# Banded attention and a gated MLP on one core: first weight loads on ScalarE's queue, one DMA queue in the plan, later second products, other buffer counts

## The chip, the cores and the metric

The kernel runs on one core of a Trainium2 chip. The metric is the time on the device in microseconds (us); one number is the median of several executions. The engines are TensorE (PE; its weight loads are listed apart as PEld), VectorE (DVE), ScalarE (ACT), GpSimd (POOL) and SyncE (SP), which here mostly issues DMAs.

## What is computed

Four batches, eight heads, 768 positions, head size 64. Each position attends to the first 4 positions (sinks) and to the last 128 positions. The result, as a matrix x of 3072 x 512, goes through an MLP of width 2048 with the Mish function between its two products.

```python
scores = scale * np.matmul(q, k.transpose(0, 1, 3, 2))
keep = is_sink | in_window
scores = np.where(keep, scores, -1e9)
a = softmax(scores); attn = np.matmul(a, v)
x = attn.transpose(0, 2, 1, 3).reshape(B * S, H * D)
h = x @ w_in                      # 3072x512 @ 512x2048
g = h * np.tanh(softplus(h))
out = g @ w_out                   # 3072x2048 @ 2048x512
```

The weights come as 64-bit numbers. The kernel turns them into float32 on the chip, from the two halves of each number, and splits each into a high and a low part.

## The kernel before

The 3072 rows are worked in 12 chunks of 256 rows. The first chunk of each batch (no rows ahead of it) comes first: these are chunks 0 to 3 in the order of work. A chunk has four pairs of heads (`pair`): products of q and k (line L387 for the first chunk of a batch, L390 for others, tiles `att`), mask and maximum on DVE (L398), exponential on ACT (L401), normalisation (L405 to L412), transposes on PE (L422), and the product with v (L440, L444).

The MLP of a chunk has eight steps (`step`), each for two of the 16 blocks of 128 hidden units. A step does its first products into the tile `hp` (L488; in "wide" steps L484 and L485, with high and low parts of x side by side, followed on DVE by a sum, L494), then a chain that alternates between ACT and DVE: exponential into the tile `u` (L497), minimum (L498), square (L499), logarithm (L500), exponential (L501), product into `n` (L502), high part `gh` (L252) and low part `gl` (L263 or L265). Then come twelve second products into two accumulators `acc` (L518). At a chunk's end the accumulators are copied out into tiles that also carry the tag `u` (L252, L254 or L537) and stored to `y` (L541). Chunks 0 to 2 go through their steps interleaved, in groups of two steps, since the weights become ready only little by little; chunks 3 to 10 run one after the other with wide steps; chunk 11 is again not wide.

Each block of weights is a DMA of 512 KB into one of three buffers `raw`, then seven or eight instructions on ACT, DVE and POOL: L288 or L289, L291, L292, L294, L296, the sum L299 or L300, the high part L252, the low part L263 or L265. After the weights, the same buffers carry pieces of k.

The order on every engine is set ahead of time by `Plan.solve`: a list scheduler with a duration for every task, a rank (`prio`), and a count of buffers by tag (`TAGS`). A task is put on the engine on which it can start first, lower rank first among equals. The engines then run exactly in this order. `emit` also puts matmuls on a zero tile (L613) into places where the plan leaves PE idle. In the plan a load takes 460 ns on SP and then 2000 ns plus 2.9 ns for each KB, whatever else is on its way. Loads that `body` issues ahead of the plan (tags in `EARLY`, lines L815 to L820) count as landed at a fixed time.

## Time and profile before

| | |
|---|---|
| median of 3 runs | 740.74 us (739.2 to 741.14) |
| the profiled execution's own time | 741.95 us |
| its span, first to last instruction | 740.2 us |
| PE busy | 723.7 us (98% of the span) |
| weight loads on PE | 609.2 us (82%) |
| DVE busy | 551.5 us (75%) |
| ACT busy | 579.5 us (78%) |
| POOL busy | 129.0 us (17%) |
| mean granted TensorE clock | 0.994 |

Busy time is the time in which an engine had an instruction under way, as a share of the span. PE's share includes the matmuls on the zero tile. What lies around the span in the execution's own time is 1.75 us.

### The profile page before, as it was taken

What the parts mean: (1) busy time and instruction counts of PE and PEld (TensorE: products, weight loads), DVE (VectorE), ACT (ScalarE), POOL (GpSimd) and SP (SyncE); (2) the same over time, 40 slices, a digit from 0 to 9 for tenths busy, and PEclk for the clock granted to TensorE, in tenths of its full rate; (3) what the DMA queues carried; (4) which work ended last, traced back from release to release, by engine and by line L of the source; (5) the groups of instructions that cost most, each with busy time, mean ns of one, the idle gap of its engine ahead of it and who ended that gap; (6) DMA issues with size and microseconds to landing.
All of it is one profiled execution on the core that took longest, in us unless ns stands there. A gap on an engine that the chain in (4) does not pass through costs nothing.

```text
span 740.2 us, 12968 instructions
## 1 busy us (share of the span) xinstructions
PE 723.7 (98%) x4466; PEld 609.2 (82%) x4466; DVE 551.5 (75%) x1415; ACT 579.5 (78%) x1293; POOL 129.0 (17%) x108
## 2 busy tenths in 40 slices
PE   7999999999999999999999999999999999999996
PEld 5578788898888888887888888888888888888995
DVE  5999989997677877668877768777777777764332
ACT  5999889778888778887778878787878778875753
POOL 1232122202042112321031130111111311100000
PEclk9999999999999999999999999999999999999999
DMA  6555334323353232223224224223313311100000
GB/s 185 172 176 154 109 120 137 121 105 88 88 149 88 73 96 89 73 75 93 75 57 127 75 57 126 58 62 109 88 44 91 97 45 34 48 18 1 31 1 33
DMA packets 48988, 64.12 MB, mean 87 GB/s; under 512 B 4880, under 2 KB 41744, under 8 KB 48912
## 3 DMA queue, kind: packets, MB, share of 16 engines
q1 hardware_dynamic: 48912, 63.20, 29.4%
q8 instruction: 37, 0.61, 0.4%
q14 instruction: 39, 0.32, 0.1%
HBM read 56.89 MB, written 6.29 MB: 85 GB/s over the span
## 4 chain that ended last, share of the span: by engine, by line
PE 72%; ACT 13%; DVE 10%; DMA 2%; issue 2%; SPq 0%; DVEq 0%; ACTq 0%
PE acc L518 29%; PE hp L484 12%; PE hp L488 9%; PE hp L485 6%; PE att L440 4%; PE att L390 4%; PE att L422 3%; ACT p L401 3%; PE att L444 2%; DVE n L494 2%; PE att L488 2%; ACT u L499 1%; ACT u L500 1%; ACT u L497 1%; ACT w L252 1%
## 5 line engine op out<-in xcount | busy, mean ns | idle before, releaser
L518 PE MATMUL acc<-w,gh 128*128 128x512 f32 x768 | 198.3, 396 | 1.5 <-ACT gh L252 1.1
L484 PE MATMUL hp<-w,w 128*128 128x512 f32 x512 | 191.9, 409 | 0.0
L518 PEld LDWEIGHTS acc<-w,gh 128*128 128x128 f32 x768 | 137.1, 189 | 30.6 <-ACT gh L252 4.4
L485 PE MATMUL hp<-w,w 128*128 128x256 f32 x512 | 143.1, 280 | 0.0
L484 PEld LDWEIGHTS hp<-w,w 128*128 128x128 f32 x512 | 96.3, 188 | 17.5 <-issue 0.2
L518 PE MATMUL acc<-w,gl 128*128 128x512 f32 x384 | 107.6, 395 | 0.0
L401 ACT ACTIVATE p<-p,nm 128x288 f32<-128x288 f32 (+1 forms) x192 | 95.6, 501 | 6.6 <-DVE nm L398 6.5
L494 DVE TENSOR_REDUCE n<-hp 128x256 f32<-128x512 f32 x128 | 87.6, 685 | 15.1 <-PE hp L485 14.6
L485 PEld LDWEIGHTS hp<-w,w 128*128 128x128 f32 x512 | 96.8, 189 | 0.6
L499 ACT ACTIVATE u<-u,bias 128x512 f32<-128x512 f32 x96 | 69.4, 724 | 34.4 <-DVE u L498 34.3
L398 DVE CUSTOM_DVE_ANT_0 p<-att,m 128x288 f32<-128x288 f32 (+2 forms) x192 | 75.2, 419 | 26.5 <-PE att L390 19.9
L488 PE MATMUL hp<-w,w 128*128 128x256 f32 x672 | 91.7, 288 | 1.9 <-DVE n L502 1.8
L488 PEld LDWEIGHTS hp<-w,w 128*128 128x128 f32 x672 | 86.0, 193 | 6.0 <-DVE n L502 2.4
L263 POOL TENSOR_TENSOR w<-raw,w 64x448 fp32r<-64x448 f32 x35 | 41.8, 1200 | 260.5 <-ACT w L252 115.5
L497 ACT ACTIVATE u<-n 128x512 f32<-128x512 f32 x64 | 40.4, 632 | 54.1 <-DVE n L494 54.0
L518 PEld LDWEIGHTS acc<-w,gl 128*128 128x128 f32 x384 | 70.9, 188 | 14.3
L498 DVE TENSOR_SCALAR u<-u 128x512 f32<-128x512 f32 x96 | 42.8, 446 | 47.2 <-ACT u L497 46.8
L252 ACT ACTIVATE gh<-n 128x512 fp32r<-128x512 f32 x94 | 58.8, 625 | 17.4 <-DVE n L502 16.8
L500 ACT ACTIVATE u<-u,bias 128x512 f32<-128x512 f32 x96 | 68.9, 719 | 1.8
L502 DVE SCALAR_TENSOR_TENSOR n<-u,n 128x512 f32<-128x512 f32 x64 | 44.5, 695 | 34.0 <-ACT u L501 33.8
L265 DVE TENSOR_TENSOR gl<-n,gh 128x512 fp32r<-128x512 f32 x75 | 53.3, 711 | 18.2 <-PE acc L518 12.9
L501 ACT ACTIVATE u<-u 128x512 f32<-128x512 f32 x96 | 60.2, 628 | 2.0
(86 smaller groups left out, 1076.1 us busy)
## 6 DMA issues: line engine op xcount, KB each, us to landing
raw<-k_p SPq DMA_DIRECT2D x64, 224.0 KB, 3.5
raw<-w_in SPq DMA_DIRECT2D x16, 512.0 KB, 3.6
raw<-w_out SPq DMA_DIRECT2D x16, 512.0 KB, 4.2
w<-q_p SPq DMA_DIRECT2D x64, 128.0 KB, 3.2
y<-u SPq DMA_DIRECT2D x24, 256.0 KB, 2.1
vt<-v_b SPq DMA_DIRECT2D x32, 192.0 KB, 2.5
vsr<-v_s SPq DMA_DIRECT2D x32, 128.0 KB, 2.3
ks<-k_p SPq DMA_DIRECT2D x16, 144.0 KB, 2.9
```

The source lines that it names most:

```text
L252: ways[ACT] = act_t(n, psum), lambda: nc.scalar.activation(dst(), src(), AF.Copy, scale=scale or 1.0)
L265: way = dve_t(n), lambda: nc.vector.tensor_tensor(dst(), a(), b(), ALU.subtract)
L398: a = add(r + .03 + .01 * e, {DVE: (dve_t(n) + 8, lambda st=st, pv=pv, nm=nm, e=e, mask=mask, n=n: nc.vector.tensor_tensor_reduce(out=pv() ...
L401: a = add(r + .05 + .01 * e, {ACT: (act_t(n, ptr=2), lambda pv=pv, nm=nm, sm=sm, e=e: nc.scalar.activation(pv(), pv(), AF.Exp, bias=nm.t[: ...
L484: yield nc.tensor.matmul(hp.t, wih[f].t[:, fs], xt, start=kt == 0, stop=False)
L485: yield nc.tensor.matmul(hp.t[:, 0, :], wil[f].t[:, fs], xt[:, 0, :], start=False, stop=kt == KT - 1)
L488: yield nc.tensor.matmul(hp.t[:, y, :], w_.t[:, fs], xt[:, z, :], start=kt == 0 and n_ == 0, stop=kt == KT - 1 and n_ == 2)
L494: hs.append(add(r + .3 + .1 * y, {DVE: (dve_t(2 * T), lambda y=y, hp=hp: nc.vector.tensor_reduce(m.t[:, y, :], hp.t.rearrange("p z t -> p ...
L499: a = add(r + .52, {ACT: (act_t(N, ptr=1), lambda: nc.scalar.activation(u.t, u.t, AF.Square, bias=self.one))}, [a], [u])
L500: a = add(r + .53, {ACT: (act_t(N, ptr=1), lambda: nc.scalar.activation(u.t, u.t, AF.Ln, bias=self.half, scale=0.5))}, [a], [u])
L501: a = add(r + .54, {ACT: (act_t(N), lambda: nc.scalar.activation(u.t, u.t, AF.Exp, scale=-1.0))}, [a], [u])
L518: yield nc.tensor.matmul(acc[t].t, g_.t[:, y, ts_], w_.t, start=new and n_ == 0, stop=done)
```

## The change

There are four parts. (1) The first three loads of weights are issued by ACT, ahead of its table load, and no longer by SP behind the loads of k, q and v. (2) The plan keeps one line of loads: each load starts 1500 ns after its issue or when the one before it is through, takes 4.5 ns for each KB, and is usable 300 ns later; the preloaded weights count as landed at 2400, 4800 and 7200 ns instead of 3000, 6000 and 9000. (3) The second products of wide steps get a rank that is 0.2 later. (4) `ks` and `qh` (k and q of the chunks at the start of a batch) have three buffers instead of two, and the third pair's loads are issued ahead of the plan; `u` has two buffers instead of three. What is computed is the same.

```diff
--- before.py
+++ after.py
@@ -51,7 +51,8 @@
 WARM, SPARE, ROOM = 14, 250, 4
 ZERO = 224
 SPL = 1.5
-EARLY = {"ks": ([P, 2 * PITCH], F32, 0), "qh": ([P, T], F32, 0), "vt": ([P, 2, 3, D], F32, 0), "raw": ([P, 512, 2], I32, 3000)}
+LINE0, LINE, SLOW = 3000, 4.5, .2
+EARLY = {"ks": ([P, 2 * PITCH], F32, 0), "qh": ([P, T], F32, 0), "vt": ([P, 2, 3, D], F32, 0), "raw": ([P, 512, 2], I32, 2400)}
 SH, QUICK = 1.0, 2
 
 
@@ -93,13 +94,13 @@
 
 
 class Task:
-    __slots__ = ("prio", "ways", "deps", "bufs", "new", "ready", "left", "start", "end", "eng", "outs", "room")
+    __slots__ = ("prio", "ways", "deps", "bufs", "new", "ready", "left", "start", "end", "eng", "outs", "room", "size")
 
     def __init__(self, prio, ways, deps, bufs, new):
         self.prio, self.ways, self.deps, self.bufs, self.new = prio, ways, deps, bufs, new
         self.ready, self.left, self.outs = dict.fromkeys(ways, 0.0), 0, []
         self.start = self.end = self.eng = None
-        self.room = 0.0
+        self.room, self.size = 0.0, 0
 
 
 class Plan:
@@ -137,7 +138,7 @@
             for d in t.deps:
                 d.outs.append(t)
         free = {e: 0.0 for e in (PE, ACT, DVE, POOL, SP)}
-        port = 0.0
+        port, line = 0.0, LINE0
         ports = lambda t, e: e == POOL or len(t.ways[e]) > 4
         pool = {e: [] for e in free}
         for t in tasks:
@@ -181,6 +182,9 @@
                 port = at + dur
             lat = t.ways[e][2] if len(t.ways[e]) > 2 else 0
             t.start, t.eng, t.end = at, e, at + dur
+            if t.size:
+                line = max(line, t.end + 1500) + t.size * LINE
+                lat = line + 300 - t.end
             free[e] = at + dur
             for x in t.ways:
                 pool[x].remove(t)
@@ -227,9 +231,9 @@
 
 
     TAGS = {
-        "ks": (2, 0), "qh": (2, 0), "vt": (2, 0), "vsr": (2, 0), "raw": (3, 0),
+        "ks": (3, 0), "qh": (3, 0), "vt": (2, 0), "vsr": (2, 0), "raw": (3, 0),
         "p2": (2, 0), "psk": (1, 0), "nm": (4, 0), "sm": (4, 0), "rc": (4, 0), "pth": (1, 0), "sks": (2, 0),
-        "u": (3, 0), "n": (2, 0), "gh": (2, 0), "gl": (1, 0), "w": (81, 0),
+        "u": (2, 0), "n": (2, 0), "gh": (2, 0), "gl": (1, 0), "w": (81, 0),
         "att": (4, 1), "hp": (2, 1), "acc": (2, 1),
     }
 
@@ -271,7 +275,12 @@
             self.c.early[buf.tag] -= 1
             k = len(self.c.first[buf.tag]) - self.c.early[buf.tag]
             return self.plan.add(prio, {SP: (1, lambda: None, EARLY[buf.tag][2] * k)}, new=[buf], **kw)
-        return self.plan.add(prio, {SP: (460, lambda: self.nc.sync.dma_start(dst(), src), 2000 + kb * 2.9)}, new=[buf], **kw)
+        return self.transfer(prio, dst, src, kb, new=[buf], **kw)
+
+    def transfer(self, prio, dst, src, kb, **kw):
+        t = self.plan.add(prio, {SP: (460, lambda: self.nc.sync.dma_start(dst(), src))}, **kw)
+        t.size = kb
+        return t
 
 
     def weights(self, f, rank):
@@ -339,7 +348,7 @@
 
         def twice(buf, t, src, kb):
             one = self.load(rank, buf, lambda: t()[up], heads(src), kb)
-            return [one, self.plan.add(rank + .01, {SP: (460, lambda: nc.sync.dma_start(t()[low], heads(src)), 2000 + kb * 2.9)}, [], [buf])]
+            return [one, self.transfer(rank + .01, lambda: t()[low], heads(src), kb, bufs=[buf])]
         half = lambda: f32(kr.t.rearrange("p n t -> p (n t)")[:, 0:2 * w]).rearrange("p (e w) -> p e w", e=2)
         ldk = twice(kr, half, self.k[b, pr, :, j0 * PITCH:j0 * PITCH + w], w / 2)
         ldq = twice(qr, lambda: qr.t, self.q[b, pr, :, i0 * P:i0 * P + T], T / 2)
@@ -516,7 +525,7 @@
                 ts_ = slice(t * P, (t + 1) * P)
                 for n_, (g_, w_) in enumerate(((gl, woh[f]),) if part else ((gh, woh[f]), (gh, wol[f]))):
                     yield nc.tensor.matmul(acc[t].t, g_.t[:, y, ts_], w_.t, start=new and n_ == 0, stop=done)
-            st.tail = add(r + 1.45 + .2 * part + (.05 * y + .1 * t if last else .1 * y + .05 * t), {PE: (pe_t(*[512] * (2 - part)), second)},
+            st.tail = add(r + 1.45 + SLOW * wide + .2 * part + (.05 * y + .1 * t if last else .1 * y + .05 * t), {PE: (pe_t(*[512] * (2 - part)), second)},
                           [gk if part else gg, st.tail] + wdeps[f][2:4], [gl if part else gh] + ([] if new else [acc[t]]), [acc[t]] if new else [])
             if done:
                 self.store(st, r, t, f2 == NF // 2 - 1)
@@ -806,18 +815,20 @@
     nc = tc.nc
     with ExitStack() as ctx:
         top = ctx.enter_context(tc.tile_pool(name="top", bufs=1))
+        held = {tag: [top.tile(shape, dtype, name=f"{tag}{i}") for i in range(Fast.TAGS[tag][0])] for tag, (shape, dtype, _) in EARLY.items()}
+        for t, src in zip(held["raw"], (w_in[0], w_out[0], w_in[1])):
+            nc.scalar.dma_start(t.rearrange("p n t -> p (n t)"), src.bitcast(I32))
         nc.scalar.preload_act_table_set("natural_log_exp_and_others")
         raw = top.tile([P, 4], I32, name="lim_raw")
         nc.sync.dma_start(raw, limits.bitcast(I32).partition_broadcast(P))
-        held = {tag: [top.tile(shape, dtype, name=f"{tag}{i}") for i in range(Fast.TAGS[tag][0])] for tag, (shape, dtype, _) in EARLY.items()}
         w = P + PITCH
         for pr in range(2):
             nc.sync.dma_start(held["ks"][pr][:, 0:w], k[0, pr, :, 0:w])
             nc.sync.dma_start(held["qh"][pr], q[0, pr, :, 0:T])
         for pr in range(2):
             nc.sync.dma_start(held["vt"][pr][:, :, 0:2, :], v[0, 2 * pr:2 * pr + 2, :, 0:2, :].rearrange("h p j d -> p h j d"))
-        for t, src in zip(held["raw"], (w_in[0], w_out[0], w_in[1])):
-            nc.sync.dma_start(t.rearrange("p n t -> p (n t)"), src.bitcast(I32))
+        nc.sync.dma_start(held["ks"][2][:, 0:w], k[0, 2, :, 0:w])
+        nc.sync.dma_start(held["qh"][2], q[0, 2, :, 0:T])
         lim = top.tile([P, 2], F32, name="lim")
         flag = top.tile([P, 1], I32, name="flag")
         with ExitStack() as c2:
```

The line numbers of the changed kernel differ: L387 becomes L396, L390 L399, L401 L410, L404 L413, L412 L421, L422 L431, L484 and L485 L493 and L494, L497 L506, L499 L508, L518 L527, L252 L256, L288 L297, L613 L622.

First place: PE at the third pair of heads of chunk 0. The tiles `ks` and `qh` carry the buffer as first digit. Before, from the second group of transposes of the first pair on:

```order
L422 MATMUL att_43_0_230<-ident_112,p2_13_0_175 128x128 x4
L387 MATMUL att_46_0_242<-ks0_61,qh0_63 128x128
L387 MATMUL att_46_1_243<-ks0_61,qh0_63 128x128
L613 LDWEIGHTS zero_87
L613 MATMUL acc_0_162<-zero_87 128x224
L613 LDWEIGHTS zero_87
L613 MATMUL acc_0_162<-zero_87 128x224
L613 LDWEIGHTS zero_87
L613 MATMUL acc_0_162<-zero_87 128x224
L440 MATMUL att_53_0_253<-pth_40_0_226,vt0_65 64x256 x2
L440 MATMUL att_53_0_253<-pth_40_0_226,vt0_65 64x128 x2
```

After, from the end of the second pair's q-k products on:

```order
L396 MATMUL att_28_0_204<-ks1_59,qh1_62 128x256
L396 MATMUL att_28_1_205<-ks1_59,qh1_62 128x256
L396 MATMUL att_34_0_217<-ks2_60,qh2_63 128x128
L396 MATMUL att_34_1_218<-ks2_60,qh2_63 128x128
L431 MATMUL att_42_0_230<-ident_116,p2_15_0_179 128x128 x2
L622 LDWEIGHTS zero_91
L622 MATMUL acc_0_166<-zero_91 128x224
L622 LDWEIGHTS zero_91
L622 MATMUL acc_0_166<-zero_91 128x224
L431 MATMUL att_47_0_239<-ident_116,p2_15_0_179 128x128 x4
```

The third pair's first products (`ks0`, `qh0`, loaded a second time, before; `ks2`, `qh2` after) moved ahead of the first pair's transposes, and the first pair's product with v now has no products on reloaded k and q ahead of it here.

Second place: ACT at the eighth block of `w_out`. `w_559` (before) and `w_575` (after) are its first piece on ACT, and `hp_517` and `hp_500` the first products of the step that stands next to it. Before:

```order
L404 ACTIVATE rc_556_0_1315<-sm_548_2_1295 128x2
L288 ACTIVATE w_559_0_1324<-raw0_67 128x512
L497 ACTIVATE u_563_0_1329<-hp_517_0_1223 128x512
L252 ACTIVATE w_567_0_1340<-acc_497_0_1192 128x512
L252 ACTIVATE w_569_0_1343<-acc_500_0_1198 128x512
L499 ACTIVATE u_563_0_1329<-u_563_0_1329,bias_104 128x512
```

After:

```order
L413 ACTIVATE rc_565_0_1334<-sm_542_1_1280 128x2
L421 ACTIVATE p2_460_0_1111<-p2_460_0_1111,rc_565_0_1334 128x256
L506 ACTIVATE u_571_0_1343<-hp_500_0_1193 128x512
L297 ACTIVATE w_575_0_1349<-raw2_68 128x512
L508 ACTIVATE u_571_0_1343<-u_571_0_1343,bias_108 128x512
L256 ACTIVATE w_584_0_1364<-acc_504_0_1204 128x512
```

The exponential into `u` stood behind the piece that needs the loaded block, and now it stands ahead of it.

Third place: PE at the start of chunk 5, a wide one; the new accumulators are `acc_2043` and `acc_2046` before, `acc_2045` and `acc_2051` after. Before:

```order
L485 MATMUL hp_2036_0_4363<-w_1935_0_4162,w_382_0_937 128x256
L518 MATMUL acc_2043_0_4381<-w_159_0_473,gh_2039_0_4371 128x512
L518 MATMUL acc_2043_0_4381<-w_181_0_516,gh_2039_0_4371 128x512
L390 MATMUL att_2045_0_4385<-w_1941_0_4175,w_1948_0_4193 128x288
L390 MATMUL att_2045_0_4385<-w_1941_0_4175,w_1957_0_4214 128x288
L390 MATMUL att_2045_1_4386<-w_1944_0_4184,w_1948_0_4193 128x288
L390 MATMUL att_2045_1_4386<-w_1944_0_4184,w_1957_0_4214 128x288
L518 MATMUL acc_2046_0_4391<-w_159_0_473,gh_2039_0_4371 128x512
L518 MATMUL acc_2046_0_4391<-w_181_0_516,gh_2039_0_4371 128x512
```

After:

```order
L494 MATMUL hp_2037_0_4369<-w_1935_0_4166,w_378_0_941 128x256
L399 MATMUL att_2043_0_4385<-w_1941_0_4179,w_1948_0_4197 128x288
L399 MATMUL att_2043_0_4385<-w_1941_0_4179,w_1957_0_4221 128x288
L399 MATMUL att_2043_1_4386<-w_1944_0_4188,w_1948_0_4197 128x288
L399 MATMUL att_2043_1_4386<-w_1944_0_4188,w_1957_0_4221 128x288
L527 MATMUL acc_2045_0_4392<-w_168_0_500,gh_2036_0_4367 128x512
L527 MATMUL acc_2045_0_4392<-w_179_0_525,gh_2036_0_4367 128x512
L431 MATMUL att_2048_0_4400<-ident_116,p2_1953_0_4209 128x128 x4
L527 MATMUL acc_2051_0_4408<-w_168_0_500,gh_2036_0_4367 128x512
L527 MATMUL acc_2051_0_4408<-w_179_0_525,gh_2036_0_4367 128x512
```

The four q-k products (L390, now L399) that stood behind the first two second products now stand ahead of them, and transposes stand between the two accumulators' first products.

## Rows read from the trace of the kernel before

**Rows 1.** Windows of chosen stretches: busy us and (instructions) of each engine, granted clock, DMA.

```profile
...
core 0: us, PE busy (x) PEld busy (x) DVE busy (x) ACT busy (x) POOL busy (x), PEclk, DMA share, GB/s
...
5.00:10.00 5.00, 4.30 (x21) 2.75 (x22) 3.08 (x22) 2.98 (x12) 0.00 (x0) 1.00 0.94 285
...
15.00:20.00 5.00, 5.00 (x31) 3.38 (x30) 2.79 (x12) 3.28 (x10) 1.28 (x1) 0.66 0.41 120
20.00:85.00 65.00, 62.50 (x456) 46.63 (x453) 63.07 (x206) 60.68 (x181) 17.12 (x13) 1.00 0.52 157
85.00:95.00 10.00, 8.38 (x60) 7.77 (x59) 8.85 (x27) 9.32 (x21) 3.43 (x3) 0.92 0.47 170
95.00:100.00 5.00, 5.00 (x25) 4.31 (x25) 3.47 (x7) 4.68 (x16) 0.39 (x1) 0.81 0.09 29
100.00:720.00 620.00, 618.64 (x3778) 528.30 (x3777) 459.95 (x1107) 487.62 (x1036) 105.45 (x83) 1.00 0.27 77
```

**Rows 2.** Waits, 5 to 20 us: waiter, what it waited for, us in total, times, longest.

```profile
...
PE att L387 <- DMA qh<-q_p: 2.2, 1, 2.2
```

**Rows 3.** Timeline of the first 15 us: start, us, engine (SPq issues DMAs), line, operation.

```profile
...
0.73 1.28 ACT L809 ACT_TABLE_LOAD   x1 [0.73 <-PEq L854]
...
3.61 0.16 DVE L834 SCALAR_TENSOR_TENSOR lim<-lim_raw 128x2 f32<-128x2 int32 x1 [1.75 <-DMA lim_raw<-limits]
...
4.05 0.47 SPq L820 DMA_DIRECT2D raw<-w_in  x1
...
6.96 0.71 PEld L387 LDWEIGHTS att<-ks,qh 64*128 64x128 f32 x4 [0.33 <-DVE nm L398]
7.00 0.40 ACT L401 ACTIVATE p<-p,nm 128x128 f32<-128x128 f32 x1 [4.99 <-DVE nm L398]
...
14.15 0.49 PE L387 MATMUL att<-ks,qh 64*128 64x128 f32 x4 [2.24 <-DMA qh<-q_p]
```

**Rows 4.** Line L816 (the first two q loads): issues and landings.

```profile
...
L816 SPq DMA_DIRECT2D qh<-q_p x2: 432/432/432, 1.6 to 2.6; - x2
...
DMA to landing us min/median/max: 2.7/3.1/3.5
```

**Rows 5.** Chain that ended last, 0 to 30 us: start us, us, what.

```profile
...
8.76 5.25 DMA qh<-q_p
...
15.03 1.48 PE att L440 x8
```

**Rows 6.** Timeline from 20 us: the same eight products, as 15.03 in rows 5.

```profile
...
20.10 0.87 PE L440 MATMUL att<-pth,vt 128*64 128x256 f32 x8
```

**Rows 7.** Waits, 85 to 95 us.

```profile
...
PE hp L488 <- DVE n L502: 1.6, 1, 1.6
```

**Rows 8.** Timeline, 86 to 93 us.

```profile
...
86.94 0.20 ACT L404 ACTIVATE rc<-sm 128x2 f32<-128x2 f32 x1
...
87.75 0.68 ACT L288 ACTIVATE w<-raw 128x512 f32<-128x512 f32 x1 [0.62 <-DMA raw<-w_out]
...
88.33 0.59 ACT L497 ACTIVATE u<-hp 128x512 f32<-128x512 f32 x1
...
92.38 0.68 DVE L502 SCALAR_TENSOR_TENSOR n<-u,hp 128x512 f32<-128x512 f32 x1
```

**Rows 9.** Waits of the weight loads on PE (PEld), 205 to 720 us.

```profile
...
PEld acc L518 <- ACT gh L252: 4.4, 11, 0.8
```

**Rows 10.** Timeline at the start of a later chunk.

```profile
...
340.63 0.58 ACT L252 ACTIVATE u<-acc 128x512 f32<-128x512 f32 x1
...
341.61 0.63 ACT L252 ACTIVATE gh<-n 128x512 fp32r<-128x512 f32 x1 [0.40 <-DVE n L502]
...
342.29 0.74 PE L518 MATMUL acc<-w,gh 128*128 128x512 f32 x2 [0.48 <-ACT gh L252]
...
342.87 0.69 PE L390 MATMUL att<-w,w 128*128 128x288 f32 x4
```

**Rows 11.** The page, part 6: one kind of DMA, KB each, median us to landing.

```profile
...
y<-u SPq DMA_DIRECT2D x24, 256.0 KB, 2.1
```

## The prediction

> **What bounds the kernel now.** I read the windows first [rows 1]. From 100 to 720 us PE is busy for 618.64 of 620 us: there the kernel is as long as its matmuls, and DVE (459.95) and ACT (487.62) have room. From 20 to 85 us it is the other way round: DVE is busy for 63.07 of 65 us and ACT for 60.68, and part of PE's 62.50 us is matmuls on the zero tile. In that stretch the conversion of the weights and the attention of the first chunks have to get through DVE and ACT, and PE gets real work as fast as they hand it over. After it PE never catches up: the matmuls that are left take as long as they take. So a microsecond counts if it lies in one of three places: on the way to a full DVE and ACT at the start, in the stretch around 90 us where PE goes over to being full, or in PE's small waits after 100 us. Idle time of DVE or ACT after 100 us is worth nothing.
>
> At the start, the reader should see in the waits that PE waited 2.2 us in one piece for a load of q [rows 2]. The timeline places it: the products for the third pair of heads start at 14.15 us [rows 3], and the chain shows the load itself, issued at 8.76 us and 5.25 us long [rows 5]. It is that late because k and q have two buffers: the third pair's load may be issued only when the first pair's products are done, and it then stands behind the weights. Right after this wait the granted clock falls: 0.66 of full over 15 to 20 us [rows 1], that is, for part of it the lower level of 1.2 GHz. Eight products with v take 1.48 us of the chain there [rows 5], and 0.87 us at the higher level at 20.10 us [rows 6].
>
> At 85 to 95 us PE is busy for 8.38 of 10 us [rows 1], and the waits name one piece of 1.6 us, for DVE's L502 [rows 7]. The timeline tells why: ACT is free at 87.14 us (86.94 + 0.20), waits for a block of w_out, works on it from 87.75, and only then does the exponential of the step, at 88.33 [rows 8]; the chain from there ends with L502 at 92.38. The clock falls again behind it: 0.92 over 85 to 95 us, 0.81 over 95 to 100 [rows 1].
>
> After 100 us, what is left are weight loads on PE that wait for gh, 11 times, 4.4 us together [rows 9].
>
> **The change part by part.**
>
> Third buffers for k and q. The third pair's products no longer need a reload, and in the new order they stand ahead of the first pair's transposes. The 2.2 us wait goes [rows 2], and with it, I take it, the slow stretch behind it: 1.48 - 0.87 = 0.6 us on the chain [rows 5, 6]. Together 2.8 us. Lower end: nothing, if DVE and ACT had been given other work meanwhile. What is late next: the third q load now waits for the first one's landing and shares the queues with 1.5 MB of weights; at PE it is wanted behind the second pair's products, around 10 us, some 4 us earlier than it was served before.
>
> Weights on ACT's queue. ACT issues three loads at some 0.47 us each [rows 3], and in the new program the third one also waits for the limits' landing (before: used at 3.61 us). The table load of 1.28 us comes behind: 3.61 + 0.47 + 1.28 = 5.4 us, and then ACT still has to read the flag. Its first exponential is at 7.00 us after 4.99 us of waiting [rows 3], so this is hidden by 1.6 us; beyond that every microsecond would be on the path. The loads of k and q are not hidden in the same way. Before, the second q was issued at 2.6 us and landed at most 3.5 us later, at 6.1 us [rows 4]; it is wanted at 6.96 us [rows 3]. Now weights flow at the same time. If the queues share evenly, as many bytes again (0.56 MB) come in between: at the 285 GB/s of 5 to 10 us [rows 1] that is 2.0 us, so it lands at 8.1 us and is 1.1 us late. If all 1.57 MB of weights went first, it would be 5.5 us more, and 4.6 us late. If the weights took only what the queue left free: nothing. A part of such a wait lies beside DVE's work on the first pair's masks, so I take 0.8 us lost, near the even share. That the weights are there sooner brings little: the first work on them stands behind the third pair's masks in the new order.
>
> This is the place where a rule speaks against the change. The row says that 285 GB/s were moved while only SP's queue was in use. The Trainium skill (DMA: Bandwidth & Descriptors, Issuing engines are not separate DMA queues) says that DMAs from ScalarE and SyncE end up on the same 16 DMA engines and interleave, and that issuing on several engines saves only the time for issuing. By that rule the change brings no transfer time and the early weights are paid for by k and q; the sum would then have the late end, 4.6 us, in the place of 0.8. No run here shows it yet.
>
> One line of loads in the plan. It changes no instruction, only their order. At the stall of 90 us it does what is wanted: the exponential stands ahead of the piece on the loaded block. It could then start at 87.14 instead of 88.33 us, 1.2 us earlier [rows 8], of the 1.6 us that PE waits. Of the low clock behind it, 10 x 0.08 + 5 x 0.19 = 1.75 us of PE's time [rows 1], I take half, 0.9, since 0.4 us of the wait remain. Bounds: 0 and 1.6 + 1.75 = 3.4 us; below nothing too, since the whole order from 20 to 95 us is another one and may stall elsewhere.
>
> Later second products. At a chunk's start [rows 10] the copy of an accumulator on ACT (340.63) delays gh (341.61 to 342.24), and PE waits 0.48 us for it. In the new order the four q-k products of 0.69 us lie in between, which is longer than that wait. Not all of the 11 places look like that one, so of the 4.4 us I take half, 2.2. Bounds 0 and 4.4.
>
> Two buffers for u. At each end of a wide chunk (8 of them) the two output tiles and the next step's u share two buffers. The next exponential, or at five ends the second output tile, then waits for the store of the first output tile, 2.1 us from issue to landing [rows 11]. At the start of chunk 5 ACT has gh (0.63) and the other copy (0.58) [rows 10] between that tile's copy and the exponential: 1.2 us are covered and 0.9 are not. Behind the exponential stand its own chain and the next pair's work on ACT, and for gh of that step PE waits last. PE has second products and q-k products in hand meanwhile, so I take 1.0 us for all eight ends together; bounds 0 (PE's work covers all) and 8 x 2.1 = 16.8 (nothing does).
>
> **Sum**, against the profiled execution (741.95 us, 740.2 of it the span): 741.95 - 2.8 + 0.8 - 1.2 - 0.9 - 2.2 + 1.0 = 736.65. That execution is 1.2 us above the median of the runs, 740.74; on the median's scale the sum is 735.4 us.
>
> **Rivals.**
> Hidden gain. DVE and ACT are full from 20 to 85 us, and they have the same instructions to do as before. If the gap at 12 to 14 us was used by them in the end, and the stall at 90 us only moves, then what is left is 2.2 - 1.0 for the wide steps, less 0.8 at the start: 740.3. For it speaks how full they are; against it, that PE's wait is in the chain that ended last [rows 5] and that their idle time ahead of 20 us is not made up anywhere.
> Late k and q. The weights push the second and third pair's loads back by 4.6 us instead of 0.8: 735.4 + 3.8 = 739.2. The rule above speaks for it; against it, that loads of two queues should get a share each.
> Slower: the exponential behind the store. If PE's cover at the chunk ends is used up and only gh's 0.63 us lies beside the store, the two buffers of u cost 8 x 1.5 = 12 us instead of 1.0: 735.4 + 11 = 746.4. From 6.3 us (0.8 at each of the eight ends) on it eats up all the rest, from 8.6 us (1.1 at each end) on the kernel is slower beyond the bound. For it: ACT runs in order, so all that stands behind the exponential waits as well. Against it: PE is full there and has work in hand.
> All of it comes. The whole of the two stalls and clock dips and of the waits for gh, with nothing lost at the start: 2.8 + 3.4 + 4.4 - 1.0 = 9.6, that is 731.1 us.
>
> **How the numbers follow.** My forecast (its own range 733 to 738.4) gets 0.52, all of it 0.08, the hidden gain 0.18, late k and q 0.09, slower 0.13. A time within 0.3% of 740.74 (738.5 to 743.0) can't be told from no change here. The forecast and the full gain are faster, and so is the better third of the two cases between 738.5 and 740.74 (0.08 of 0.27): 0.68. The rest of those two, 0.19, is no change, and 0.13 is slower. The range leaves out the outer half of the full gain and the slower case: 731 to 742 us.
>
> **What would show it.** In the new profile, the third pair's q-k products should stand at 10 to 11 us instead of 14.15, with no wait on a load over 1 us, and no clock of 0.66 over 15 to 20 us. The second pair's products should start before 8 us; later means that the weights took its bandwidth. ACT's first exponential should stay at 7.0 to 7.5 us. Between 85 and 100 us there should be no PE wait over 1 us and no clock of 0.81. After 100 us weight loads should wait for gh for about 2 us in all. If instead the waits list ACT's exponential, L506, or the copies of accumulators behind DMAs of y, the buffers of u were the mistake; if DVE and ACT are full but PE has its new waits elsewhere between 30 and 95 us, the plan's new order is.

## The result and the profile after

The changed kernel takes 735.18 us (median of 6 runs, 734.82 to 735.92), the kernel before 740.58 us (6 runs); the ratio is 0.9926, with a 95% interval of 0.9911 to 0.9941. That is 5.5 us less, and the forecast was 735.4. The profiled execution took 734.82 us with a span of 732.8, against 741.95 and 740.2. The size came out as forecast, but not by the steps that were forecast: one term was a quarter of what it should have been, one gain lay in another place than forecast, and the errors of the sizes cancelled.

The windows of the new kernel, with the columns of [rows 1]:

```profile
...
5.00:10.00 5.00, 1.31 (x8) 1.00 (x9) 2.31 (x15) 1.28 (x1) 0.00 (x0) 1.00 1.05 388
10.00:15.00 5.00, 4.60 (x31) 3.21 (x29) 3.93 (x26) 4.58 (x19) 0.00 (x0) 1.00 0.77 227
15.00:20.00 5.00, 4.94 (x40) 3.17 (x42) 4.78 (x23) 5.00 (x18) 0.06 (x1) 1.00 0.28 82
20.00:85.00 65.00, 61.64 (x459) 46.60 (x456) 63.26 (x209) 62.87 (x188) 18.89 (x14) 1.00 0.55 167
85.00:95.00 10.00, 10.00 (x68) 8.87 (x67) 9.93 (x25) 9.60 (x23) 2.55 (x2) 1.00 0.42 138
95.00:100.00 5.00, 5.00 (x34) 3.88 (x33) 4.94 (x11) 4.68 (x8) 0.00 (x0) 1.00 0.09 22
100.00:720.00 620.00, 619.81 (x3797) 531.01 (x3795) 451.45 (x1106) 478.60 (x1031) 111.24 (x85) 1.00 0.27 76
```

Three things are to be seen against [rows 1]. From 5 to 10 us DVE and ACT did less than before (2.31 against 3.08, 1.28 against 2.98), while the DMA engines moved more (388 GB/s against 285): the start got worse. From 15 to 20 us DVE is busy for 4.78 us where it was 2.79, and ACT for all 5.00 where it was 3.28, at the full clock: the gap at the third pair is closed. From 85 to 100 us PE has no idle time and no low clock, and after 100 us it is busy for 619.81 us where it was 618.64.

The waits of the first 20 us say what the start waits for:

```profile
...
ACT L821 <- DMA lim_raw<-limits: 6.3, 1, 6.3
...
PE att L396 <- DMA qh<-q_p: 4.9, 1, 4.9
DVE lim L845 <- DMA lim_raw<-limits: 4.1, 1, 4.1
```

And the timeline, for the same places as [rows 3]:

```profile
...
0.73 0.40 ACTq L820 DMA_DIRECT2D raw<-w_in  x1
0.74 0.39 SPq L823 DMA_DIRECT2D lim_raw<-limits  x1
...
5.92 0.33 ACTq L820 DMA_DIRECT2D raw<-w_in  x1
5.92 0.16 DVE L845 SCALAR_TENSOR_TENSOR lim<-lim_raw 128x2 f32<-128x2 int32 x1 [4.06 <-DMA lim_raw<-limits]
...
6.28 1.28 ACT L821 ACT_TABLE_LOAD   x1 [6.28 <-DMA lim_raw<-limits]
...
7.61 0.23 DVE L809 COPY m<-m 128x128 f32<-128x128 f32 x1
...
8.69 2.27 PE L396 MATMUL att<-ks,qh 64*128 64x128 f32 x12 [4.86 <-DMA qh<-q_p]
...
9.95 0.70 PEld L396 LDWEIGHTS att<-ks,qh 64*128 64x128 f32 x4 [0.34 <-DVE nm L407]
10.00 0.40 ACT L410 ACTIVATE p<-p,nm 128x128 f32<-128x128 f32 x1 [2.44 <-DVE nm L407]
...
11.56 1.39 PE L396 MATMUL att<-ks,qh 64*128 64x256 f32 x8
```

DVE has the limits at 5.92 us instead of 3.61 and ends the masks at 7.84 (7.61 + 0.23), and PE has the first pair's k and q at 8.69 us; the second pair's products stand at 9.95 instead of 6.96 and ACT's first exponential at 10.00 instead of 7.00. The whole opening is 3.0 us late. The DMA issues show it as well: lim_raw has 2 KB, and it took 5.2 us to land (2.8 before); the first two blocks of weights, issued on ACT's queue at 0.73 and 1.17 us, took 5.8 and 7.1, and the third was issued only at 5.92 us (the 5.5 below is the median of the first and the third).

```profile
...
raw<-w_in ACTq DMA_DIRECT2D x2, 512.0 KB, 5.5
raw<-w_out ACTq DMA_DIRECT2D x1, 512.0 KB, 7.1
lim_raw<-limits SPq DMA_DIRECT2D x1, 2.0 KB, 5.2
```

The third pair's products come directly behind the second pair's (the eight products from 11.56 us on are half of the one and half of the other) and wait for no load.

Past 205 us the weight loads of the second products hardly wait for gh any more, 0.7 us where [rows 9] had 4.4:

```profile
...
PEld acc L527 <- ACT gh L256: 0.7, 2, 0.4
```

The row of the stores of y gives a milestone that all kernels here have in common: its first and last issue. Before and after:

```profile
...
L541 SPq DMA_DIRECT2D y<-u x24: 332/346/1985, 188.1 to 735.0; - x24
```

```profile
...
L550 SPq DMA_DIRECT2D y<-u x24: 332/346/356, 183.8 to 727.9; - x24
...
who waited for it (us, times):
  ACT u L506: 1.0, 1
```

So 4.3 us were gained ahead of the first store (188.1 to 183.8), and 2.8 from there to the last (546.9 to 544.1). The two profiled executions are 7.1 us apart, the medians 5.5. And of the eight ends of wide chunks one has ACT's exponential waiting for a store, for 1.0 us.

### The profile page after: what moved, and what is told of

The parts are those of the page before. It is cut to its first block, busy times and chain, and to the rows that moved or that the text cites. A ratio compares the mean times of both kernels' runs of the same rounds, so it can differ in the third digit from the quotient of the medians.

```text
span 732.8 us, 12975 instructions
## 1 busy us (share of the span) xinstructions
PE 717.3 (98%) x4468; PEld 605.3 (83%) x4468; DVE 543.9 (74%) x1419; ACT 569.8 (78%) x1288; POOL 134.0 (18%) x109
## 4 chain that ended last, share of the span: by engine, by line
PE 90%; DVE 4%; ACT 4%; DMA 1%; issue 1%; SPq 0%; ACTq 0%; DVEq 0%
PE acc L527 35%; PE hp L493 16%; PE hp L497 10%; PE hp L494 8%; PE att L449 5%; PE att L399 4%; PE att L431 4%; PE att L453 3%; PE att L497 2%; ACT p L410 1%; PE att L396 1%; DMA qh<-q_p 1%; ACT p L421 1%; DVE p L407 1%; ACT w L256 1%; DVE w L305 1%
## 5 line engine op out<-in xcount | busy, mean ns | idle before, releaser
L527 PE MATMUL acc<-w,gh 128*128 128x512 f32 x768 | 198.4, 396 | 0.2 <-ACT gh L256 0.2
L493 PE MATMUL hp<-w,w 128*128 128x512 f32 x512 | 192.1, 409 | 0.0
L527 PEld LDWEIGHTS acc<-w,gh 128*128 128x128 f32 x768 | 136.1, 188 | 26.3 <-ACT gh L256 0.8
L494 PE MATMUL hp<-w,w 128*128 128x256 f32 x512 | 143.3, 280 | 0.0
L493 PEld LDWEIGHTS hp<-w,w 128*128 128x128 f32 x512 | 96.3, 188 | 17.1 <-issue 0.2
L527 PE MATMUL acc<-w,gl 128*128 128x512 f32 x384 | 108.3, 390 | 0.0
L410 ACT ACTIVATE p<-p,nm 128x288 f32<-128x288 f32 (+1 forms) x192 | 95.3, 499 | 3.6 <-DVE nm L407 3.5
L494 PEld LDWEIGHTS hp<-w,w 128*128 128x128 f32 x512 | 96.8, 189 | 1.5
L407 DVE CUSTOM_DVE_ANT_0 p<-att,m 128x288 f32<-128x288 f32 (+1 forms) x192 | 74.6, 419 | 25.2 <-PE att L399 20.2
L508 ACT ACTIVATE u<-u,bias 128x512 f32<-128x512 f32 x96 | 69.0, 720 | 29.8 <-DVE u L507 29.8
L497 PE MATMUL hp<-w,w 128*128 128x256 f32 x672 | 89.6, 285 | 0.2 <-DVE n L511 0.2
L497 PEld LDWEIGHTS hp<-w,w 128*128 128x128 f32 x672 | 84.9, 191 | 3.9 <-issue 0.5
L527 PEld LDWEIGHTS acc<-w,gl 128*128 128x128 f32 x384 | 71.9, 188 | 14.1
L506 ACT ACTIVATE u<-n 128x512 f32<-128x512 f32 x64 | 40.5, 632 | 54.1 <-DVE n L503 54.1
L267 POOL TENSOR_TENSOR gl<-n,gh 128x512 fp32r<-128x512 f32 x32 | 41.4, 1293 | 202.6 <-ACT gh L256 173.1
L256 ACT ACTIVATE gh<-n 128x512 fp32r<-128x512 f32 x93 | 58.3, 626 | 20.4 <-DVE n L511 20.3
L507 DVE TENSOR_SCALAR u<-u 128x512 f32<-128x512 f32 x96 | 44.7, 466 | 38.2 <-ACT u L506 37.6
L269 DVE TENSOR_TENSOR gl<-n,gh 128x512 fp32r<-128x512 f32 x64 | 48.2, 754 | 15.4 <-PE acc L527 12.2
```

The costliest lines, as they stand in the source:

```text
L256: ways[ACT] = act_t(n, psum), lambda: nc.scalar.activation(dst(), src(), AF.Copy, scale=scale or 1.0)
L269: way = dve_t(n), lambda: nc.vector.tensor_tensor(dst(), a(), b(), ALU.subtract)
L407: a = add(r + .03 + .01 * e, {DVE: (dve_t(n) + 8, lambda st=st, pv=pv, nm=nm, e=e, mask=mask, n=n: nc.vector.tensor_tensor_reduce(out=pv() ...
L410: a = add(r + .05 + .01 * e, {ACT: (act_t(n, ptr=2), lambda pv=pv, nm=nm, sm=sm, e=e: nc.scalar.activation(pv(), pv(), AF.Exp, bias=nm.t[: ...
L493: yield nc.tensor.matmul(hp.t, wih[f].t[:, fs], xt, start=kt == 0, stop=False)
L494: yield nc.tensor.matmul(hp.t[:, 0, :], wil[f].t[:, fs], xt[:, 0, :], start=False, stop=kt == KT - 1)
```

## The experiments

The parts of the change were undone one at a time in the changed kernel, and made one at a time in the kernel before. The kernel before took 740.1 to 741.17 us (medians) on the chips used, so kernels are compared by their ratio to the kernel before on the same chip; "gain" is (1 - ratio) x 740.6 us. An interval reaches 0.6 to 1.2 us to either side, so a difference of two gains is known to about 1.5 us. The five kernels whose names begin with f are the kernel before with lines of one part of the change's diff and no others. The new landing times of the preloaded weights (2400 instead of 3000 ns) stand in all kernels that begin with e and in none that begin with f; no run tries them by themselves. The last three columns come from each kernel's trace: when PE starts on the first products of k and q, when the third pair's products start (with three buffers: when the eight products do that they are in), the first store of y, and the time from there to the last store.

| kernel | ratio (95%) | gain us | first, third pair | first store | to the last |
|---|---|---|---|---|---|
| before | 1 | 0 | 5.70, 14.15 | 188.1 | 546.9 |
| changed | 0.9926 (0.9911 to 0.9941) | 5.5 | 8.69, 11.56 | 183.8 | 544.1 |
| changed, weights on SP (e1_sp) | 0.9884 (0.9868 to 0.9899) | 8.6 | 5.70, 8.57 | 181.3 | 543.9 |
| changed, weights behind ACT's table load (e2_late) | 0.9920 (0.9906 to 0.9934) | 5.9 | 8.52, 11.39 | 183.7 | 544.0 |
| changed, SLOW = 0 (e3_slow0) | 0.9965 (0.9953 to 0.9977) | 2.6 | 8.73, 11.59 | 184.5 | 546.8 |
| changed, old price of a load (e4_lat) | 0.9955 (0.9942 to 0.9968) | 3.3 | 8.62, 11.49 | 187.1 | 544.0 |
| changed, two k and q (e5_kq2) | 0.9931 (0.9918 to 0.9944) | 5.1 | 8.70, 15.86 | 186.4 | 543.6 |
| changed, three u (e6_u3) | 0.9913 (0.9900 to 0.9927) | 6.4 | 8.48, 11.35 | 184.1 | 542.9 |
| changed, weights on SP, three u (e7_best) | 0.9855 (0.9840 to 0.9870) | 10.7 | 5.70, 8.57 | 181.2 | 542.9 |
| before, weights on ACT (f5_actw) | 0.9991 (0.9983 to 1.0000) | 0.7 | 8.76, 14.79 | 187.6 | 546.9 |
| before, two u (f1_u2) | 1.0012 (1.0001 to 1.0024) | -0.9 | 5.70, 13.96 | 186.7 | 546.8 |
| before, later second products (f2_slow) | 0.9955 (0.9938 to 0.9971) | 3.3 | 5.69, 14.29 | 187.2 | 542.9 |
| before, one line (f3_line) | 0.9966 (0.9954 to 0.9978) | 2.5 | 5.67, 14.08 | 184.5 | 546.1 |
| before, three k and q (f4_kq3) | 0.9968 (0.9955 to 0.9982) | 2.4 | 5.70, 8.57 | 183.7 | 547.1 |

The first stores of before, f1 and f2 are of the same order of work up to there: 188.1, 186.7 and 187.2. A difference of 1.4 us in that column says nothing.

**Weights back on SP (e1_sp).** My theory after the result was that the weights' bytes push the limits, k and q back, and that this lateness stays to the end; the rivals, that it is made up, or that the weights are wanted early.

```diff
-        for t, src in zip(held["raw"], (w_in[0], w_out[0], w_in[1])):
-            nc.scalar.dma_start(t.rearrange("p n t -> p (n t)"), src.bitcast(I32))
...
         nc.sync.dma_start(held["qh"][2], q[0, 2, :, 0:T])
+        for t, src in zip(held["raw"], (w_in[0], w_out[0], w_in[1])):
+            nc.sync.dma_start(t.rearrange("p n t -> p (n t)"), src.bitcast(I32))
```

> The changed kernel with the three loads of weights back on SP, behind the third pair's k and q; PE, DVE, POOL and the rest of ACT keep their order instruction for instruction. My theory: the weights on ACT's queue push the limits' landing from 3.6 to 5.9 us and the first k and q behind it, so the whole opening is 3.0 us late and, since DVE is nearly full from 10 us on, most of it stays to the end. Then ACT's first exponential is at about 7.0 us again and the time is 2 to 3 us below the changed kernel's 735.2: about 732.5. Rival one, the late start is made up before 100 us: first exponential at 7.0, time 735 all the same. Rival two, the weights are needed where they now are: DVE or ACT wait over 1 us for a block of weights before 20 us, and the time is 735 to 737.

It took 731.99 us. Its timeline:

```profile
...
3.62 0.16 DVE L845 SCALAR_TENSOR_TENSOR lim<-lim_raw 128x2 f32<-128x2 int32 x1 [1.76 <-DMA lim_raw<-limits]
...
5.04 0.43 SPq L831 DMA_DIRECT2D raw<-w_in  x1
...
5.70 2.26 PE L396 MATMUL att<-ks,qh 64*128 64x128 f32 x12 [1.87 <-DVE m L809]
...
7.01 0.40 ACT L410 ACTIVATE p<-p,nm 128x128 f32<-128x128 f32 x1 [4.99 <-DVE nm L407]
...
8.57 1.65 PE L396 MATMUL att<-ks,qh 64*128 64x256 f32 x8
```

The same instructions in the same order on PE, DVE and POOL: the limits are back at 3.62 us, the weights are issued from 5.04 us on, nothing waits for them, and the time is 3.1 us less by the ratios (2.7 by the two spans, 732.8 and 730.1): about all of the 3.0 us of the start come back at the end. Both rivals fall.

**Weights behind the table load (e2_late).** In e1_sp the table load is early too, so it might have been ACT's lateness and not the bytes.

```diff
+        nc.scalar.preload_act_table_set("natural_log_exp_and_others")
         for t, src in zip(held["raw"], (w_in[0], w_out[0], w_in[1])):
             nc.scalar.dma_start(t.rearrange("p n t -> p (n t)"), src.bitcast(I32))
-        nc.scalar.preload_act_table_set("natural_log_exp_and_others")
```

> The changed kernel with ACT's three loads of weights behind its table load (issued from about 2.0 us instead of 0.7); nothing else moves. My theory (the transfers share the DMA engines): the limits, issued at 0.74, land at about 3.5 us, the first pair's k and q are late by 1 us or less, the second pair's more; first exponential at 7.5 to 8.5 us, time 733 to 734. Rival, it is ACT's late table load behind the third weight load that delays the first exponential and not the bytes: then the first exponential is at 7.0 and the time about 732.5, as with the weights on SP. Rival two, nothing of the opening counts: 735.

```profile
...
0.73 1.28 ACT L819 ACT_TABLE_LOAD   x1 [0.73 <-PEq L865]
...
0.76 0.39 ACTq L821 DMA_DIRECT2D raw<-w_in  x1
...
5.44 0.16 DVE L845 SCALAR_TENSOR_TENSOR lim<-lim_raw 128x2 f32<-128x2 int32 x1 [3.58 <-DMA lim_raw<-limits]
...
8.52 2.26 PE L396 MATMUL att<-ks,qh 64*128 64x128 f32 x12 [4.69 <-DMA qh<-q_p]
...
9.83 0.40 ACT L410 ACTIVATE p<-p,nm 128x128 f32<-128x128 f32 x1 [7.82 <-DVE nm L407]
```

The expected delay of the weights did not come: the first was issued at 0.76 us, during the table load that stands ahead of it in the program, not at 2.0. But the run tells the two causes apart all the same: the table is loaded at 2.01 us, and the first exponential still stands at 9.83, because PE gets k and q at 8.52. It is the transfers. The late table load costs nothing in the changed kernel: it is over at 7.56 us (6.28 + 1.28), 2.44 us before the first exponential; the 0.17 us between the two runs stand at PE's start already (8.69 and 8.52).

**Weights on ACT alone (f5_actw).** The same move of the weights in the kernel before; the plan keeps its 3000 ns for them, so that no order changes.

```diff
+        for t, src in zip(held["raw"], (w_in[0], w_out[0], w_in[1])):
+            nc.scalar.dma_start(t.rearrange("p n t -> p (n t)"), src.bitcast(I32))
         nc.scalar.preload_act_table_set("natural_log_exp_and_others")
...
-        for t, src in zip(held["raw"], (w_in[0], w_out[0], w_in[1])):
-            nc.sync.dma_start(t.rearrange("p n t -> p (n t)"), src.bitcast(I32))
```

> The kernel before with the first three weight loads on ACT's queue ahead of the table load, nothing else; every engine's order stays. My theory: limits, k and q are late as in the changed kernel, first exponential at 10.0 instead of 7.0 us. The third pair's reload is then issued at about 11.8 instead of 8.8 us, but no longer behind weights: 3 us instead of 5.25, so its products start at about 15 instead of 14.15, and the time is 1 us longer, 741.5. Rival, all of the 3.0 us stays on the path: 743.5.

It was not 1 us slower: 0.9991. The timeline:

```profile
...
8.76 2.26 PE L387 MATMUL att<-ks,qh 64*128 64x128 f32 x12 [4.93 <-SPq L884]
...
10.45 0.33 SPq L274 DMA_DIRECT2D ks<-k_p  x1
...
10.88 0.37 SPq L274 DMA_DIRECT2D qh<-q_p  x1
...
14.79 0.49 PE L387 MATMUL att<-ks,qh 64*128 64x128 f32 x4
```

And these two loads in the list of DMAs, with KB and us to landing:

```profile
...
ks<-k_p SPq DMA_DIRECT2D x1, 144.0 KB, 2.2
qh<-q_p SPq DMA_DIRECT2D x1, 128.0 KB, 2.0
```

The opening is 3 us late here as well, but the reload of the third pair's k and q is issued 10.45 and 10.88 us after the start with no weights ahead of it, takes 2.2 and 2.0 us (q before: 5.25, [rows 5]) and is there in time: the products start at 14.79 us, 0.6 later than before, without a wait for it. In the kernel before the reload sets the pace, and the weights pay their cost back there. With the third buffers nothing pays it back.

**Two buffers for k and q again (e5_kq2), and three alone (f4_kq3).**

```diff
-        "ks": (3, 0), "qh": (3, 0), "vt": (2, 0), "vsr": (2, 0), "raw": (3, 0),
+        "ks": (2, 0), "qh": (2, 0), "vt": (2, 0), "vsr": (2, 0), "raw": (3, 0),
...
-        nc.sync.dma_start(held["ks"][2][:, 0:w], k[0, 2, :, 0:w])
-        nc.sync.dma_start(held["qh"][2], q[0, 2, :, 0:T])
```

> The changed kernel with two buffers for k and q and without the third pair's early loads: part of part 4 undone. By the prediction's term of 2.8 us the time is 738.0; PE's third pair waits for a reloaded q again, until about 14.5 us, and the clock falls behind it. Rival, since the first products are 3 us late already, the reload is issued late but finds the queues free: the third pair's products start 1 us later at most and the time is 735 to 736.

f4_kq3 adds the same lines to the kernel before, with the third pair's loads ahead of the weights:

```diff
-        "ks": (2, 0), "qh": (2, 0), "vt": (2, 0), "vsr": (2, 0), "raw": (3, 0),
+        "ks": (3, 0), "qh": (3, 0), "vt": (2, 0), "vsr": (2, 0), "raw": (3, 0),
...
+        nc.sync.dma_start(held["ks"][2][:, 0:w], k[0, 2, :, 0:w])
+        nc.sync.dma_start(held["qh"][2], q[0, 2, :, 0:T])
         for t, src in zip(held["raw"], (w_in[0], w_out[0], w_in[1])):
```

> The kernel before with three buffers for k and q and the third pair's loads ahead of the weights on SP, nothing else (u keeps three, the plan its old price of a load). By the prediction's term it gains 2.8 us: 737.9, with the third pair's products at about 9 us and the first store of y at 185.3. By the two kernels with weights on ACT and the old price of a load (first store at 187.1 with third buffers, 187.6 without) it gains 0.5: 740.1. If that is so, the gains of the line and of the buffers only come together: 6.8 us for both, by the changed kernel with the weights on SP.

With the weights on ACT the third buffers are worth 0.4 us by the ratios and 1.1 by the medians, which can't be told from nothing: nearer to the rival. The third pair's products do start 4.3 us later (15.86 against 11.56), not 1 us, but PE does not wait for the reload, and the clock does not fall (1.00 from 15 to 20 us). Alone, with the weights on SP, 2.4: the prediction's 2.8. The waits of e5_kq2 from 85 to 95 us, and that window of f4_kq3, hold the finding that I had not expected:

```profile
...
PE hp L497 <- DVE n L511: 1.5, 1, 1.5
```

```profile
...
20.00:85.00 65.00, 62.84 (x467) 49.47 (x468) 63.27 (x207) 60.40 (x173) 15.64 (x12) 1.00 0.52 159
85.00:95.00 10.00, 10.00 (x66) 8.81 (x66) 10.00 (x20) 9.02 (x17) 1.28 (x1) 1.00 0.43 142
```

The stall at 90 us is there in every kernel with two buffers (before, f1, f2, f3, f5, e5) and in none with three, with the one line or without it. What in the order of work removes it is not shown.

**Old price of a load (e4_lat), and the one line alone (f3_line).**

```diff
-                line = max(line, t.end + 1500) + t.size * LINE
-                lat = line + 300 - t.end
+                lat = 2000 + t.size * 2.9
```

> The changed kernel with the plan's old price of a load (2000 ns + 2.9 ns per KB, each load by itself) in place of the one line: part 2 alone undone, and with it the order from the start on. By the prediction's terms (-1.2 for the stall at 90 us and -0.9 for the clock dip behind it) the time goes up by 2.1 us to 737.3, with a PE wait of 1 us or more and a granted clock below 0.95 somewhere between 85 and 100 us. Rival: the stall was a chance of that one order and any new order loses it; then there is no such wait and the time is 735.2 within 1 us.

> The kernel before with the one line of loads in the plan, nothing else. By the prediction's terms it gains 2.1 us: 738.5, with no stall at 90 us. By the first store of y in the changed kernel without third buffers (186.4 us) against the kernel before with weights on ACT (187.6) it gains 1.2 us: 739.5. Rival: without the third buffers the wait for the reloaded q at 14 us remains and swallows it: 740.6.

Undone the line costs 2.1 us by the ratios, and alone it brings 2.5: the size of the prediction. But e4_lat has PE busy for 10.00 of 10 us from 85 to 95, and f3_line still has the stall. What the line takes away shows in part in ACT's waits from 20 to 100 us of e4_lat (this one ends at 97.72 us), and in the window of 20 to 85 us:

```profile
...
ACT w L296 <- DMA raw<-w_out: 1.2, 1, 1.2
```

```profile
...
20.00:85.00 65.00, 62.02 (x468) 47.98 (x465) 63.03 (x211) 60.05 (x175) 16.93 (x13) 1.00 0.51 153
85.00:95.00 10.00, 10.00 (x64) 8.67 (x63) 10.00 (x20) 9.41 (x20) 1.29 (x1) 1.00 0.55 168
```

With the line no kernel has a listed wait of ACT for a block of weights from 20 to 100 us; without it each has one or two (0.5 to 1.3 us in all), all between 87 and 98 us. From 20 to 85 us no kernel has one, but ACT is busy for 62.10 to 63.43 of the 65 us in the eight kernels with the line and for 60.05 to 60.72 in the six without; in e4_lat it waits there for DVE and PE. So with the line ACT gets more done before 85 us, and how that comes to 2.1 us at the end is not shown.

**SLOW = 0 (e3_slow0), and later second products alone (f2_slow).**

```diff
-LINE0, LINE, SLOW = 3000, 4.5, .2
+LINE0, LINE, SLOW = 3000, 4.5, 0
```

> The changed kernel with SLOW = 0: part 3 alone undone, the order up to chunk 1's end unchanged. My theory: the weight loads of second products wait for gh for about 4 us in all after 100 us again instead of 0.7, and the time is 2.2 to 2.5 us longer, 737.5. Rival, the waits for gh only stood beside other small gaps of PE: the waits come back in the list and the time stays at 735.2 within 1 us.

> The kernel before with the second products of wide steps 0.2 later in rank, nothing else. By the prediction's term it gains 2.2 us: 738.5. By the runs so far (542.9 us from the first store to the last in the changed kernel with three buffers of u, 546.9 before) it gains 4.0 us: 736.7, with the waits for gh at 0.7 us or less instead of 4.4.

Undone it costs 2.9 us by the ratios (2.7 from the first store to the last, 2.8 by the medians), alone it brings 3.3. With SLOW = 0 the waits for gh are back:

```profile
...
PEld acc L527 <- ACT gh L256: 3.7, 8, 0.8
```

In f2_slow no such row is left. It also bears on the clock. Its waits for DVE's L502 from 5 to 100 us, of which the one of 1.3 us is the stall, and its windows around 90 us:

```profile
...
PE hp L488 <- DVE n L502: 1.5, 2, 1.3
```

```profile
...
85.00:95.00 10.00, 8.69 (x66) 7.98 (x65) 9.14 (x29) 9.74 (x21) 3.79 (x3) 1.00 0.51 169
95.00:100.00 5.00, 5.00 (x29) 4.38 (x28) 4.23 (x9) 4.12 (x14) 0.07 (x1) 1.00 0.13 46
```

The stall is there as in [rows 7], but the clock behind it is 1.00; so it is in f1_u2, f3_line, f5_actw and e5_kq2. Of six traces with the stall only [rows 1] has the dip of 0.92 and 0.81, so the stall alone does not bring it. That a fallen clock costs nothing in the kernel before does not follow: of its 21 executions on the chip of f1 to f4, the two with a mean granted clock of 0.998 and 1.000 took 738.12 and 738.31 us, the eight at 0.994 or less 739.56 to 741.91. f4_kq3 had 0.997 to 1.000 in all nine of its executions and took 736.23 to 738.31, so a part of its gain may be a clock that falls less often; how much is open.

**Three buffers for u (e6_u3), and two alone (f1_u2).**

```diff
-        "u": (2, 0), "n": (2, 0), "gh": (2, 0), "gl": (1, 0), "w": (81, 0),
+        "u": (3, 0), "n": (2, 0), "gh": (2, 0), "gl": (1, 0), "w": (81, 0),
```

> The changed kernel with three buffers for u, as before the change; the order differs from chunk 1 on. The term of the prediction for two buffers was +1.0 us, so this should be 734.2. The new trace shows no wait for a store of y, which says that two buffers cost nothing: 735.2 within 0.7. Rival, two buffers cost what the slower case said, 6 us or more: then 729 or less.

> The kernel before with two buffers for u, nothing else; the order differs from chunk 1 on. By the prediction's term it is 1.0 us slower: 741.7. But with SLOW = 0 in the changed kernel the time from the first store of y to the last was 546.8 us, and 546.9 in the kernel before, which had three buffers: by that, two buffers cost nothing here and the time is 740.7 within 0.5.

Three buffers bring 1.0 us by the ratio and 1.1 by the medians, and 1.2 from the first store to the last; two alone cost 0.9, which is about what can't be told from nothing, and the stores show no loss there (546.8). The column "to the last" says when they cost: 542.9 us in all three kernels with later second products and three buffers, 543.6 to 544.1 with two. It is not the wait for a store, of which the changed kernel has one (the expectation of e6_u3 says none): where it stands (691.71 us), PE is busy for 15.00 of the 15 us from 685 to 700. PE at the end of a chunk, in the changed kernel and in e6_u3:

```profile
...
207.62 0.35 PE L622 MATMUL acc<-zero 128*128 128x224 bf16 x2
208.13 0.73 PE L527 MATMUL acc<-w,gh 128*128 128x512 f32 x2 [0.15 <-ACT gh L256]
```

```profile
...
207.82 0.27 PE L440 MATMUL att<-ident,psk 128*128 128x128 f32 x1
207.85 0.47 PE L493 MATMUL hp<-w,w 128*128 128x512 f32 x1
...
210.02 2.00 PE L527 MATMUL acc<-w,gh 128*128 128x512 f32 x8
```

With two buffers the plan has nothing for PE ahead of the new chunk's second products but two matmuls on the zero tile (L622), and a wait for gh: 0.5 us. With three it has first products there. The other half I have not located.

**Both costs taken out (e7_best).** The edits of e1_sp and e6_u3 together.

> The changed kernel with the weights on SP and three buffers for u, that is, without the two parts that cost. If the gains of the two (3.2 and 1.1 us) lie in different places, as the traces say (before 20 us, and at the ends of wide chunks), they add up: 730.9. If part of the one hides the other: 731.5 to 732.

730.82 us, 0.9855 of the kernel before: 10.7 us less, and 5.2 less than the change as it was made, by the ratios (4.4 by the medians). The two gains add up, and this is the best version.

## Why the forecast came out, step by step

- **What bounds it.** Right. The start, the stretch up to 100 us and PE's small waits behind it are where the gains and losses were found, as far as they were found.
- **Third buffers, -2.8.** Near in size as a part by itself (-2.4, f4_kq3), the wait for the reloaded q gone; but that gain includes the stall at 90 us, which the prediction had put to the line. The 0.6 us for the slow stretch behind the wait is not bound to the wait: f3_line waits 2.4 us for the same q, and its clock is 1.00 from 15 to 20 us. As part of this change the buffers were worth 0.4 to 1.1 (e5_kq2), because the weights on ACT's queue had already made the reload fast (2.0 us for q in f5_actw).
- **Weights on ACT's queue, +0.8.** This step failed. "Near the even share" gave 1.1 us of lateness for the second q alone, and took the limits at 3.61 us as given. The limits and the very first k and q, issued at the same time as the weights, were late, the whole opening by 3.0 us. DVE's work on the masks did not cover it, since the masks need the limits (they end at 7.84 instead of 5.52 us), and the first q came later still, at 8.69. Measured: +3.1 in company of the third buffers (e1_sp). By itself a gain of 0.7 us, hardly to be told from nothing (f5_actw, 0.9983 to 1.0000): what the move costs depends on the buffers.
- **One line of loads, -1.2 and -0.9.** The size is right (2.1 undone, 2.5 alone), the place is wrong. The step "the exponential stands ahead of the piece on the loaded block, so the stall shrinks" failed: the stall goes with the third buffers, with the line or without. What the line did was to keep ACT busier from 20 to 85 us (62.87 us instead of 60.05 in e4_lat) and to take away its wait of 1.2 us for a block of weights at 97.72 us; how this adds up to 2.1 us stays open. The 0.9 us for the clock was read from one execution, and five other traces have the stall without the dip.
- **Later second products, -2.2.** The mechanism is right, the term too small: 2.9 to 3.3. I took half of the 4.4 us of waits for gh; 3.7 of them went.
- **Two buffers for u, +1.0.** The size is right (1.0), the mechanism is not: the waits for stores that I counted are there once, and cost PE nothing; half of the loss, at the one chunk's end that was looked at, is in what the plan puts there, and the rest is not located.
- **The sum.** From the changed kernel, undone: weights +3.1, later second products -2.9, u +1.0, which leaves, of the 5.5 us gained, 6.7 for third buffers and line together, where the forecast had 4.9. Alone they brought 2.4 and 2.5, also 4.9; e7_best against f2_slow, which has neither, gives 7.4 for both. So they seem to be worth more together than apart, by little more than the intervals allow; why is not shown. The start was 2.3 us worse than forecast, and the rest 2.5 better; so the sum was right by luck, its errors cancelling.
- **The rivals.** "Late k and q" was right in its mechanism: the second pair's products stood at 9.95 us, past the 8 us that the prediction named, the third pair's behind 11.56 instead of at 10 to 11, and the first exponential at 10.00 instead of 7.0 to 7.5. The rule of the Trainium skill (DMA: Bandwidth & Descriptors, Issuing engines are not separate DMA queues), that DMAs issued by ScalarE and SyncE end up on the same 16 DMA engines and interleave, agrees with the trace: the 16 DMA engines were busy all through 5 to 10 us (share 1.05, 388 GB/s), and a load of 2 KB took 5.2 us instead of 2.8. The rival's price of 4.6 us was 1.5 too high (it took all three blocks of weights, and the third was issued only at 5.92 us), and the other parts gave 2.5 more; by these two its time of 739.2 was too long. "Hidden gain" (740.3) and "behind the store" (746.4) fell with the time, 735.2. "All of it comes" (731.1, with nothing lost at the start) fell for this kernel, too; with the weights on SP it took 731.99.

## What to carry to other kernels

A load that is issued early on another engine's queue was not free here: it shared the DMA engines with the small loads that the first instruction waits for, so issue what is needed first, and the large loads behind it. What a part of a change costs depends on which wait ends last beside it: the same move of three loads cost nothing in the kernel before and 3.1 us once the buffers had taken the wait away that hid it; so each part is to be tried with and without the others. And a sum that comes out right proves none of its terms. A dip of the clock in one profile is no term of a sum before other executions show it.

## What was not expected of the hardware

- A load of 2 KB took 5.2 us from issue to landing, against 2.8 before, with two loads of 512 KB issued on another queue at 0.73 and 1.17 us.
- ACT issued its DMAs at 0.76 and 1.18 us, while its table load, ahead of them in the program, ran from 0.73 to 2.01 us (e2_late).
- The granted clock in the first 20 us differs between kernels whose first products stand at the same time: over 10 to 15 us it was 1.00 in the changed kernel and 0.54 in e4_lat (nearly all of it at the lower level of 1.2 GHz), with first products at 8.69 and 8.62 us and DVE and ACT busy for 3.93 and 4.58, 3.48 and 4.28 us. Nor does a 1.00 there tell the speed: e6_u3 has 1.00 as well, and yet two transposes at 13.19 us take 0.66 us, as in e4_lat (0.66 at 13.32) and not as in the changed kernel (0.41 at 13.35). No run here shows what sets it.
